# Heads grouped by parity in a memory-attention kernel: scores and the group-0 fold on 64x32 tiles

## The chip, the core and the metric

The kernel runs on one core of a Trainium2 chip. The metric is the device time of one execution, in microseconds (us). TensorE is called PE below (PEld is its weight load), VectorE DVE, ScalarE ACT, GpSimd POOL, and SyncE SP.

## The reference

Attention through 32 memory slots for each of 4 batches and 8 heads, then two dense stages; all of it in float32 (`q`, `k`, `v`: 4 x 8 x 576 x 64, `phi`: 4 x 8 x 576 x 32):

```
a   = softmax(phi, axis=2)                    # over the tokens
k_m = einsum('bhsm,bhsd->bhmd', a, k)         # 32 x 64 for each head
v_m = einsum('bhsm,bhsd->bhmd', a, v)
p   = softmax(q @ k_m^T / 8, axis=-1)         # scores: 576 x 32 for each head
x   = (p @ v_m), heads side by side           # 2304 x 512
x   = ((x @ w_a) * (x @ w_b)) @ w_out         # 512 -> 1536 -> 512
h   = x @ w_in                                # 512 -> 2048
out = (h * sigmoid(1.702 h)) @ w_out2         # 2048 -> 512
```

## The kernel before

The kernel never forms `p @ v_m`. It keeps the attention weights `p` (32 slots x 8 heads = 256 rows for a batch, two halves of 128) and multiplies the values into `w_a` and `w_b`: for each group `g` of 256 columns of F1 (six groups) and each batch, `eff = v_m @ [w_a | w_b]` is made by a fold, and `gated(g, b, u)` multiplies `eff` by `p` (u is a half of the 576 tokens). `proj(g, b, u)` then multiplies by `w_out` and sums over the groups. The second dense stage (L1148, L1349, L1380) follows. The dense matmuls take each float32 operand as a high and a low part in three passes (PASSES).

The heads are cut into NHG = 2 groups of HG = 4. Attention runs over n = 0 to 7, n = 2 b + group. `memory(n)` takes `phi` to the softmax, makes the normalised keys and values of its four heads (L578, `kvn` L592), transposes them (L600) and copies them out of PSUM into two tiles: `bdk` for the keys and `bdv` for the values. Both are written so that a 128-row weight holds one head of 64 rows and 64 rows of zeros; POOL cleared them at the start (L1549). The scores are two groups of matmuls (L622, e = 0 and 1, the two token halves that lie in the upper and lower 64 rows of `qT`), each with four weights of 128 x 32, one for each head, into the four 32-row strips of one PSUM bank. DVE transposes each of the two banks (L628), and `softmax` goes on from there. `queries(n)` loads `q` as one 128-row DMA (L350) and transposes it into `qT`.

The fold of group 0 (`fold0(b)`, L756) has for each half c of the heads four matmuls with weights of 128 x 32 from `bdv`, moving the 512 columns of a decoded weight tile `wab` (the tile of row block r holds heads 2r and 2r + 1). With four heads in order in a half, half c needs the row blocks 2c and 2c + 1. `fold_out` takes the result out: ACT makes the high part (L814), DVE the low part (L816), then the bank is free. The folds of the groups 1 to 5 (`fold(g, pb)`, L800, ten calls of 16 matmuls, two batches each) take a copy of the values (`bdw`, made by `move_memory`) by slices of 64 rows and 32 columns.

PSUM has eight banks in two pools: `bank_m` for the dense work (three banks) and `bank_a` for the attention (five). `warm_up` takes one of `bank_m` at the start and keeps it until the first projections' inputs are there; it fills PE with products of the identity (L1442, the last at L1444). `lend_banks` moves two banks from `bank_a` to `bank_m` when the first half of n = 1 is done, and `close_attention` moves the rest.

The order of all instructions is written by a planner (`Order`): each stream yields the engine, the earliest time and the duration of its next step; the planner takes the step that can start first (in steps of 40 ns, then by priority), on the clocks of its own cost model. `main` has priority 50 and sets the order of the dense work; attention has 10 and up, `warm_up` 99. A step on PE can start 70 ns after its inputs' time (`_plan`), and a step that draws from a pool waits for a bank.

DMAs of `phi`, `kv`, `q` and the packed weights (`raw`) go out on SP in the order FIRST and then by need. A packed weight tile is decoded by ACT (L420) and DVE or POOL (L422 to L435) into `dm` tiles.

Of the kernel before, what the change touches and what calls it, by code (L numbers as in the profile page):

```python
# [176 lines left out]
def tile_mem_attention_moe_moe2(  # L177
# [56 lines left out]
    def slots(pl, n, shape, name, dt=F32):  # L234
# [3 lines left out]
    w2d = dram.tile([F2, DM], F32, name="w2d")  # L238

    banks = [psum.tile([P, 512], F32, name=f"bank{i}") for i in range(8)]  # L240
    bank_m, bank_a = Slots(banks[:3]), Slots(banks[3:])
    raw_s = slots(wp, 2, [P, 512, 2], "raw", U32)
    raw_x = slots(pa, 1, [P, 512, 2], "raw_x", U32)
    raw_p = slots(pa, 1, [P, 512, 2], "raw_p", U32).free[0]
# [14 lines left out]
        g1_m[:, i * G1 * 2 * U:(i + 1) * G1 * 2 * U].rearrange("p (j i t) -> p j i t", j=G1, i=2) for i in range(3)  # L259
    ])  # L260
    p2 = tc.alloc_tile_pool(name="p2", bufs=1)
    bdv_m = p2.tile([P, B * H * M], F32, name="bdv")
    bdv = [
        bdv_m[:, b * H * M:(b + 1) * H * M].rearrange("p (r m) -> p r m", r=H // 2) for b in range(B)
    ]
    gr_s = slots(p2, 3, [P, U], "gr")
    dm_x = slots(p2, 1, [P, 512], "dm_x").free
    dm_s.free += dm_x
    ident = pa.tile([P, P], F32, name="ident")
    zero = pa.tile([P, 1], F32, name="zero")  # L270
    bdk = [pa.tile([P, HG, 2, M], F32, name=f"bdk{i}") for i in range(2)]
    eff_p = pa.tile([P, 2, 2 * CW], F32R, name="eff_p")
    phi_s = slots(pa, 2, [P, HG, C0, M], "phi")
    et_s = slots(pa, 1, [P, C0, SP, 2], "et")
# [40 lines left out]

    def load_heads(dst, src, n, queue=nc.sync):
        b, g = divmod(n, NHG)
        rows_ = src[b, g * HG:(g + 1) * HG].rearrange("h (p c) d -> p h c d", c=SC)
        queue.dma_start(out=dst[0::2], in_=rows_[:, :, :C0, :])
        queue.dma_start(out=dst[1::2, :, :SC - C0, :], in_=rows_[:, :, C0:, :])  # L320

# [3 lines left out]
    def load(x, n):  # L325
        if x == "raw":
            s = yield "slot", raw_of(n)
            if s is raw_p and n >= RX:

                od.mark(s[1], "raw_p")  # L330
                s = yield "slot", raw_of(n)
            srcs, runs = pieces[n][2:]
            m = 512 // len(srcs)
            for i, src in enumerate(srcs):
                dst = s[0][:, i * m:(i + 1) * m, :]
                (nc.scalar if n < 1 else nc.sync).dma_start(
                    out=dst.rearrange("p (n f) w -> p n (f w)", n=runs), in_=src
                )
            size = P * 4096
        else:  # L340
            s = yield "slot", {"phi": phi_s, "kv": kv_s, "q": q_s}[x]
            if x == "kv":
                for i, src in enumerate((k, v)):
                    load_heads(s[0][:, i], src, n)
            elif x == "phi":
                load_heads(s[0], phi, n, nc.scalar if n == 1 else nc.sync)
            else:
                b, g = divmod(n, NHG)
                src = q[b, g * HG:(g + 1) * HG].rearrange("h (p c) d -> (h p) (c d)", c=QC)
                nc.sync.dma_start(out=s[0].rearrange("p c d -> p (c d)"), in_=src)  # L350
            size = HG * S * {"phi": M, "kv": 2 * D, "q": D}[x] * 4
        loaded[x, n] = s
        od.load(s[1], size, x, n)
# [17 lines left out]
        pieces += [(("in", g), i, [rows(w_in, 2 * i, 2, g * G2 * P, G2 * P)], 2) for i in range(2)]  # L371
    pieces += [(("o2", c), 0, [rows(w_o2, c, 1, 0, DM)], 1) for c in range(F2 // P)]
    slots_of = {"o1": whl_s}
    NWB = 10
    decoded = {}

    def decode(first, last, prio):
# [103 lines left out]

    qT_t = {}

    def row(b, h):

        return (h + b % 2) % HG * M

    def queries(n):
        t = yield "mark", "q", n
# [23 lines left out]
    def memory(n):  # L513
# [86 lines left out]
            nc.tensor.transpose(kt[:, i, :], kvn[0][:, i].rearrange("p u d -> p (u d)"), ident)  # L600
        kvn_s.release(kvn, t)
        bk = bdk[n % 2]
        for o in range(2):
            half = slice(o * D, (o + 1) * D)
            t1 = yield from copy(t, bk[half, :, o, :], kt[half, 0, :].rearrange("p (h m) -> p h m", m=M), 128)
        for o in range(2):
            half = slice(o * D, (o + 1) * D)
            t2 = yield from copy(
                t, bdv[b][half, 2 * g:2 * g + 2, o * M:(o + 1) * M],
                kt[half, 1, :].rearrange("p (r o m) -> p r o m", o=2, m=M)[:, :, o, :], 64,  # L610
            )
        bank_a.release(ps, t2)
        od.mark(t2, "bdv", n)

        t = max(t1, (yield "mark", "qT", n))
        qT = qT_t.pop(n)
        sT = yield "slot", sT_s
        ends = []
        for e in range(2):
            t1, ps = yield PE, t, 560, bank_a  # L620
            for h in range(HG):
                nc.tensor.matmul(  # L622
                    ps[0][row(b, h):row(b, h) + M, :U], bk[:, h, e, :], qT[0][:, h, :], start=True, stop=True
                )
            if e == 1:
                qT_s.release(qT, t1)
            t1, _ = yield DVE, max(t1, sT[1]), dve(U)
            nc.vector.transpose(out=sT[0][:, e * U:(e + 1) * U], in_=ps[0][:, :U])  # L628
            bank_a.release(ps, t1)
            ends.append(t1)  # L630
# [56 lines left out]
    def close_attention():  # L687

        for n in range(NU):
            for e in range(2):  # L690
                yield "mark", "attn", n, e
        for c in range(NHG):
            yield "mark", "eff", 0, B - 1, c
        yield "mark", "issued", 0, B - 2, 1
        yield "mark", "raw_p"
        for s in list(bank_a.free):
            bank_m.free.append(s)
        pa.release()
        measured()
        nonlocal py, pz, pv  # L700
        py = tc.alloc_tile_pool(name="py", bufs=1, side="right", reuse_waits="tile")
        pz = tc.alloc_tile_pool(name="pz", bufs=1, side="right", reuse_waits="tile")
        n, nw = 4 * CW, 2 * CW
        big["y0"] = y0 = py.tile([P, 7 * 4 * N2 + 8], F32R, name="y0")
        big["eff_b"] = eff_b = pz.tile([P, NHG * n], F32R, name="eff_b")
        big["whl_b"] = whl_b = pz.tile([P, 4 * G1 * CW], F32R, name="whl_b")
        whl_s.free.append([whl_b, 0.0])
        pv = tc.alloc_tile_pool(name="pw", bufs=1, side="right", reuse_waits="tile")
        plain = pv.tile([P, (NWB * 2 + 4) * CW], F32, name="plain")
        give(wab_s, views(plain, nw, NWB))  # L710

        def effs(*flat):
            return [x.rearrange("p (i f) -> p i f", i=2) for x in flat]

        eff_t.append(effs(*(eff_b[:, c * n:(c + 1) * n] for c in range(NHG))))
        eff_t.append(effs(g1_m[:, :n], g1_m[:, n:2 * n]))
        eff_t.append(effs(g1_m[:, 2 * n:3 * n], y0[:, 2 * G1 * NT:2 * G1 * NT + n]))
        for i in (HI, LO):
            flat = y0[:, i * G1 * NT:(i + 1) * G1 * NT]
            eff_y.append(effs(*(flat[:, c * n:(c + 1) * n] for c in range(NHG))))  # L720
            g1_all.append(flat.rearrange("p (j t) -> p j t", j=G1))
        bdw.extend(x.rearrange("p (r m) -> p r m", r=H // 2) for x in views(plain, H * M, B, NWB * nw))
        od.spawn(8, move_memory())


# [22 lines left out]
    def fold0(b):  # L748
        for c in range(NHG):
            t = yield "mark", "bdv", b * NHG + c  # L750
            for r in range(2):
                t = max(t, (yield "mark", "wab", 0, 2 * c + r, 0))
            t, ps = yield PE, t, 880, bank_m
            for h in range(HG):
                r, k = divmod(h, 2)
                nc.tensor.matmul(  # L756
                    ps[0][row(b, h):row(b, h) + M, :], bdv[b][:, 2 * c + r, k * M:(k + 1) * M],
                    wt["wab", 0, 2 * c + r][0], start=True, stop=True,
                )
            od.spawn(0, fold_out(t, 0, b, c, ps))  # L760

    def move_memory():

        for b in range(B):
            t = 0.0
            for c in range(NHG):
                t = max(t, (yield "mark", "bdv", b * NHG + c))
            t, e = yield {POOL: pool(H * M), ACT: act(H * M)}, t
            dst, src = (x[b].rearrange("p r m -> p (r m)") for x in (bdw, bdv))
            if e == POOL:  # L770
                nc.gpsimd.tensor_copy(dst, src)
            else:
                nc.scalar.activation(out=dst, in_=src, func=AF.Copy)
            od.mark(t, "bdw", b)
        more = [[bdv_m[:, i * 512:(i + 1) * 512], t] for i in range(2)]
        dm_x.extend(more)
        dm_s.free += more

    def fold(g, pb):

# [6 lines left out]
        for i in range(2):  # L787
            for c in range(NHG):
                t, ps[i, c] = yield PE, t - HOP_PE, FOLD if len(ps) == 3 else 0.0, bank_m


        for k in range(NHG):
            for z in (k, 1 - k):
                c, rows_ = k if z == 0 else 1 - k, slice(z * D, (z + 1) * D)
                for h in (z, z + 2):
                    r = 2 * c + h // 2
                    for i in range(2):
                        b = 2 * pb + i
                        o = row(b, h)
                        nc.tensor.matmul(  # L800
                            ps[i, c][0][o:o + M, :], bdw[b][rows_, r, z * M:(z + 1) * M],
                            wt["wab", g, r][0][rows_, :], start=True, stop=True,
                        )
        if pb == B // 2 - 1:
            for r in range(2 * NHG):
                (dm_s if g == 1 else wab_s).release(wt["wab", g, r], t)
# [733 lines left out]
    with tc.manual_schedule():  # L1540
# [4 lines left out]
        for t in [zero, *unused]:  # L1545
            nc.vector.memset(t, 0.0)
        make_identity(nc, ident)
        for t in [*bdk, *bdv]:
            nc.gpsimd.memset(t, 0.0)  # L1549
        n0 = 2 * NHG  # L1550
        od.spawn(0, load_all(FIRST))

# [47 lines left out]
```

## Time and profile before

| what | value |
|---|---|
| median of 3 runs | 774.17 us (773.63 to 2647.37) |
| the profiled execution | 773.3 us |
| its span | 771.5 us |
| PE busy | 760.2 us (99%) |
| PEld busy | 691.2 us (90%) |
| DVE busy | 602.4 us (78%) |
| ACT busy | 382.7 us (50%) |
| POOL busy | 343.2 us (44%) |
| share of PE in the chain that ended last | 93% |

The span is what the trace covers; 1.8 us of the profiled execution lie around it. Busy times are sums over a span of several stages, so the table tells which engine is loaded and not which wait ends last in a stage. A float32 matmul stands in the trace as two MATMUL records, so a group of four matmuls is x8. The end of a matmul is modelled, so the distance from one start to the next is the measure of what a group takes on PE.

### The profile page before, as it was taken

To read this page: it belongs to the slowest core of one execution; us is meant where nothing else is said; L and a number is where in the kernel's file an instruction comes from. 1 tells how busy PE (TensorE), PEld (TensorE's weight loads), DVE (VectorE), ACT (ScalarE), POOL (GpSimd) and SP (SyncE) were. 2 spreads that over 40 slices of the span, in tenths; PEclk is the share of its full clock that TensorE was granted. 3 is DMA by queue.
4 is the path that set the end of the run, shared out by engine and by line. 5 is a ranking of instruction groups with operands and counts; after the bars stand their busy time and mean duration, and the time that the engine had idled before them with its cause. 6 is when DMAs were issued, how large, how long until landed. Compare 5 with 4: busy or idle time off the path is not lost.

```text
span 771.5 us, 14636 instructions
## 1 busy us (share of the span) xinstructions
PE 760.2 (99%) x5448; PEld 691.2 (90%) x5448; DVE 602.4 (78%) x1084; ACT 382.7 (50%) x858; POOL 343.2 (44%) x329
## 2 busy tenths in 40 slices
PE   8999999999999999999999999999999999999997
PEld 7777788999988988989999999999998888889997
DVE  4888989888977897347999878777797887647886
ACT  4567766453434344235565555454554455434442
POOL 1223214444235533226698655433271047654563
PEclk9999999999999999999999999999999999999999
DMA  8956502332221332000012546454679955824421
GB/s 293 329 181 199 162 28 88 106 110 82 83 82 31 107 110 82 1 1 3 1 59 100 184 146 189 157 178 150 219 241 345 294 152 175 265 69 137 137 77 35
DMA packets 70183, 103.97 MB, mean 135 GB/s; under 512 B 5856, under 2 KB 48864, under 8 KB 70112
## 3 DMA queue, kind: packets, MB, share of 16 engines
q1 hardware_dynamic: 64656, 93.64, 38.0%
q10 hardware_dynamic: 5456, 9.41, 3.5%
q8 instruction: 42, 0.69, 0.4%
q14 instruction: 29, 0.24, 0.1%
HBM read 75.24 MB, written 27.79 MB: 134 GB/s over the span
## 4 chain that ended last, share of the span: by engine, by line
PE 93%; DVE 3%; DMA 2%; ACT 1%; issue 1%; SPq 0%; ACTq 0%; DVEq 0%
PE bank L1148 23%; PE bank L840 19%; PE bank L1349 14%; PE bank L1380 10%; PE bank L873 10%; PE bank L896 10%; PE bank L800 2%; DMA phi<-in_phi_dram 1%; PE bank L622 1%; PE bank L578 1%; DMA kv<-in_v_dram 1%; PE bank L497 1%; PE bank L756 1%; ACT et L550 0%; DVE mx L544 0%
## 5 line engine op out<-in xcount | busy, mean ns | idle before, releaser
L304 POOL TENSOR_TENSOR acc<-acc 128x512 f32<-128x512 f32 (+2 forms) x64 | 81.8, 1292 | 81.1 <-ACT y L310 32.3
L304 DVE TENSOR_TENSOR attn<-acc,attn 128x512 fp32r<-128x512 f32 (+2 forms) x93 | 89.4, 981 | 32.1 <-ACT attn L310 32.0
L1190 DVE TENSOR_TENSOR acc<-bank,acc 128x384 f32<-128x384 f32 x168 | 89.4, 552 | 29.8 <-PE bank L1148 19.3
L310 ACT ACTIVATE attn<-acc 128x512 fp32r<-128x512 f32 (+2 forms) x114 | 67.1, 603 | 55.3 <-PE bank L1380 17.9
L853 ACT ACTIVATE gr<-bank 128x288 f32<-128x288 f32 x96 | 38.9, 406 | 76.4 <-PE bank L840 60.4
L1200 ACT ACTIVATE acc<-acc 128x384 f32<-128x384 f32 x96 | 49.0, 522 | 50.8 <-DVE acc L1190 49.8
L304 POOL TENSOR_TENSOR y<-gr,y 128x288 fp32r<-128x288 f32 x44 | 37.5, 855 | 77.6 <-ACT y L310 77.5
L856 DVE TENSOR_TENSOR gr<-bank,gr 128x288 f32<-128x288 f32 x96 | 43.2, 452 | 31.5 <-PE bank L840 26.1
L840 PE MATMUL bank<-attn,eff 128*128 128x288 f32 x384 | 54.6, 297 | 0.0
L840 PEld LDWEIGHTS bank<-attn,eff 128*128 128x128 f32 x384 | 52.0, 188 | 2.9 <-issue 0.9
L873 PEld LDWEIGHTS bank<-g,whl_b 128*128 128x128 f32 x384 | 51.4, 188 | 1.7 <-ACT g L310 1.7
L873 PE MATMUL bank<-g,whl_b 128*128 128x288 f32 x384 | 52.7, 296 | 0.0
L1148 PE MATMUL bank<-attn,y 128*128 128x384 f32 x288 | 52.3, 335 | 0.0
L896 PE MATMUL bank<-y,whl_a 128*128 128x512 f32 (+1 forms) x240 | 51.6, 370 | 0.0
L896 PEld LDWEIGHTS bank<-y,whl_a 128*128 128x128 f32 x240 | 41.4, 188 | 9.8 <-ACT y L310 2.5
L1148 PEld LDWEIGHTS bank<-attn,y 128*128 128x128 f32 x288 | 50.1, 188 | 0.0
L916 DVE TENSOR_TENSOR acc<-bank,acc 128x512 f32<-128x512 f32 (+1 forms) x72 | 38.4, 552 | 13.4 <-PE bank L896 12.8
L304 POOL TENSOR_TENSOR g<-gr,g 128x288 fp32r<-128x288 f32 x28 | 26.3, 941 | 39.2 <-ACT g L310 38.8
L1349 PE MATMUL bank<-wv,attn 128*128 128x512 f32 x180 | 43.2, 394 | 0.0
L1349 PEld LDWEIGHTS bank<-wv,attn 128*128 128x128 f32 x180 | 33.9, 188 | 7.6
L840 PE MATMUL bank<-attn,eff_b 128*128 128x288 f32 x288 | 40.0, 295 | 0.0
L422 POOL TENSOR_SCALAR plain<-plain 128x512 f32<-128x512 f32 x15 | 24.5, 1636 | 34.3 <-ACT plain L420 34.3
(272 smaller groups left out, 1876.4 us busy)
## 6 DMA issues: line engine op xcount, KB each, us to landing
g2d<-acc SPq DMA_DIRECT2D x96, 192.0 KB, 1.9
raw<-in_moe_w_out_dram SPq DMA_DIRECT2D x28, 512.0 KB, 4.3
acc<-g2d SPq DMA_DIRECT2D x10, 1024.0 KB, 5.4
raw<-in_moe_w_in_dram SPq DMA_DIRECT2D x16, 512.0 KB, 3.7
acc<-g2d SPq DMA_DIRECT2D x16, 512.0 KB, 5.4
raw<-in_moe_w_a_dram SPq DMA_DIRECT2D x20, 256.0 KB, 2.8
raw<-in_moe_w_b_dram SPq DMA_DIRECT2D x20, 256.0 KB, 3.1
q<-in_q_dram SPq DMA_DIRECT2D x8, 576.0 KB, 6.4
```

The source lines that it names most:

```text
L304: (nc.gpsimd if e == POOL else nc.vector).tensor_tensor(out=dst, in0=in0, in1=in1, op=op)
L310: nc.scalar.activation(out=hi, in_=src, func=AF.Copy)
L840: nc.tensor.matmul(ps[0][:, :U], e[c][:, sw, i * CW + j * P:i * CW + (j + 1) * P], attn(b, mv, c, u * U, U), start=(n == 0), stop=(n == 3 ...
L853: nc.scalar.activation(out=gr[0], in_=pa_[0][:, :U], func=AF.Copy)
L856: nc.vector.tensor_tensor(out=gr[0], in0=pb[0][:, :U], in1=gr[0], op=ALU.mult)
L873: nc.tensor.matmul(ps[0][:, :U], w[:, sw, j, mb * P:(mb + 1) * P], g1[0][:, j, mv, :], start=(n == 0), stop=(n == 3 * G1 - 1),)
L896: nc.tensor.matmul(ps[0][:, :e - o], w[:, sw, j, mb * P:(mb + 1) * P], g1_all[mv][:, j, o:e], start=(n == 0), stop=(n == 3 * G1 - 1),)
L1148: nc.tensor.matmul(ps[0][:, :N2], w[:, sw, r, :], y[mv][r], start=(n == 0), stop=(n == 5))
L1190: nc.vector.tensor_tensor(out=s[0], in0=ps[0][:, :N2], in1=x[0], op=ALU.add)
L1200: nc.scalar.activation(out=c[0], in_=c[0], func=AF.Gelu_apprx_sigmoid)
L1349: nc.tensor.matmul(ps[i, s][0], b[0][:, sw, c - o, :], wo2[c][:, mv], start=(c == n == 0), stop=(c == 4 * K4 - 1 and n == 2),)
L1380: nc.tensor.matmul(ps[name][0][:, :NB], x[0][:, sw, c, :], moving(b, h // 2 + c, mv), start=(h == c == n == 0), stop=(h > 0 and c == K4 - ...
```

## The change

Head h now belongs to group h mod 2, so group g holds the heads g, g + 2, g + 4, g + 6. A half of the fold's rows then has one head in each row block, always in the same 64 rows. One copy of the keys (`bk`, in both 64-row halves as the transpose leaves it, one copy of 128 x 128) and one of the values (64 x 128 into the half g of `bdv`) replace the two and two copies; the zeros and their clearing go. The scores of both token halves are issued together, eight weights of 64 x 32 into two banks. `fold0` takes for half c the rows 64 c to 64 c + 63 of all four row blocks; the steps of its two halves follow each other, the first with no duration in the planner's model. `fold` of the other groups uses the same helper `fold_head`, so the order of its 16 matmuls differs. The pools are now two and six banks. `q` goes out as four DMAs of 32 rows, since the heads of a group no longer lie side by side. `bdv` is half as wide, which makes room for one more `dm_x` tile from the start (one fewer later) and for an eleventh decoded weight tile (NWB).

```diff
-    bank_m, bank_a = Slots(banks[:3]), Slots(banks[3:])
+    bank_m, bank_a = Slots(banks[:2]), Slots(banks[2:])
...
-    bdv_m = p2.tile([P, B * H * M], F32, name="bdv")
+    bdv_m = p2.tile([P, B * HG * M], F32, name="bdv")
...
-    dm_x = slots(p2, 1, [P, 512], "dm_x").free
+    dm_x = slots(p2, 2, [P, 512], "dm_x").free
...
-    bdk = [pa.tile([P, HG, 2, M], F32, name=f"bdk{i}") for i in range(2)]
+    bdk = [pa.tile([P, HG * M], F32, name=f"bdk{i}") for i in range(2)]
...
-        rows_ = src[b, g * HG:(g + 1) * HG].rearrange("h (p c) d -> p h c d", c=SC)
+        rows_ = src[b].rearrange("(h g) (p c) d -> g p h c d", g=NHG, c=SC)[g]
...
-                src = q[b, g * HG:(g + 1) * HG].rearrange("h (p c) d -> (h p) (c d)", c=QC)
-                nc.sync.dma_start(out=s[0].rearrange("p c d -> p (c d)"), in_=src)
+                src = q[b].rearrange("(h g) (p c) d -> g h p (c d)", g=NHG, c=QC)[g]
+                for h in range(HG):
+                    nc.sync.dma_start(
+                        out=s[0][h * QP:(h + 1) * QP].rearrange("p c d -> p (c d)"), in_=src[h]
+                    )
...
-    NWB = 10
+    NWB = 11
...
-        for o in range(2):
-            half = slice(o * D, (o + 1) * D)
-            t1 = yield from copy(t, bk[half, :, o, :], kt[half, 0, :].rearrange("p (h m) -> p h m", m=M), 128)
-        for o in range(2):
-            half = slice(o * D, (o + 1) * D)
-            t2 = yield from copy(
-                t, bdv[b][half, 2 * g:2 * g + 2, o * M:(o + 1) * M],
-                kt[half, 1, :].rearrange("p (r o m) -> p r o m", o=2, m=M)[:, :, o, :], 64,
-            )
-        bank_a.release(ps, t2)
+        t1 = yield from copy(t, bk, kt[:, 0, :], 128)
+        half = slice(g * D, (g + 1) * D)
+        t2 = yield from copy(t, bdv[b][half].rearrange("p r m -> p (r m)"), kt[half, 1, :], 128)
+        bank_a.release(ps, max(t1, t2))
...
+        t, p0 = yield PE, t, 0.0, bank_a
+        t, p1_ = yield PE, t - HOP_PE, 560, bank_a
+        for h in range(HG):
+            for e, ps in enumerate((p0, p1_)):
+                rows_ = slice(e * D, (e + 1) * D)
+                nc.tensor.matmul(
+                    ps[0][row(h), :U], bk[rows_, h * M:(h + 1) * M], qT[0][rows_, h, :], start=True, stop=True
+                )
+        qT_s.release(qT, t)
         ends = []
-        for e in range(2):
-            t1, ps = yield PE, t, 560, bank_a
-            for h in range(HG):
-                nc.tensor.matmul(
-                    ps[0][row(b, h):row(b, h) + M, :U], bk[:, h, e, :], qT[0][:, h, :], start=True, stop=True
-                )
-            if e == 1:
-                qT_s.release(qT, t1)
-            t1, _ = yield DVE, max(t1, sT[1]), dve(U)
+        for e, ps in enumerate((p0, p1_)):
+            t1, _ = yield DVE, max(t, sT[1]), dve(U)
...
     def fold0(b):
         for c in range(NHG):
             t = yield "mark", "bdv", b * NHG + c
-            for r in range(2):
-                t = max(t, (yield "mark", "wab", 0, 2 * c + r, 0))
-            t, ps = yield PE, t, 880, bank_m
-            for h in range(HG):
-                r, k = divmod(h, 2)
-                nc.tensor.matmul(
-                    ps[0][row(b, h):row(b, h) + M, :], bdv[b][:, 2 * c + r, k * M:(k + 1) * M],
-                    wt["wab", 0, 2 * c + r][0], start=True, stop=True,
-                )
-            od.spawn(0, fold_out(t, 0, b, c, ps))
+            for r in range(2 * NHG):
+                t = max(t, (yield "mark", "wab", 0, r, 0))
+            t, ps = yield PE, t - c * HOP_PE, (0.0, FOLD / 2)[c], bank_m
+            fold_head(c, bdv[b], 0, ps)
+            od.spawn(0, fold_out(t if c else t + FOLD / 2, 0, b, c, ps))
+
+    def fold_head(c, mem, g, ps):
+        half = slice(c * D, (c + 1) * D)
+        for h in range(HG):
+            nc.tensor.matmul(
+                ps[0][row(h), :], mem[half, h, :], wt["wab", g, h][0][half, :], start=True, stop=True
+            )
...
-        more = [[bdv_m[:, i * 512:(i + 1) * 512], t] for i in range(2)]
-        dm_x.extend(more)
-        dm_s.free += more
+        more = [bdv_m, t]
+        dm_x.append(more)
+        dm_s.free.append(more)
...
-        for k in range(NHG):
-            for z in (k, 1 - k):
-                c, rows_ = k if z == 0 else 1 - k, slice(z * D, (z + 1) * D)
-                for h in (z, z + 2):
-                    r = 2 * c + h // 2
-                    for i in range(2):
-                        b = 2 * pb + i
-                        o = row(b, h)
-                        nc.tensor.matmul(
-                            ps[i, c][0][o:o + M, :], bdw[b][rows_, r, z * M:(z + 1) * M],
-                            wt["wab", g, r][0][rows_, :], start=True, stop=True,
-                        )
+        for i in range(2):
+            for c in range(NHG):
+                fold_head(c, bdw[2 * pb + i], g, ps[i, c])
...
-        for t in [*bdk, *bdv]:
-            nc.gpsimd.memset(t, 0.0)
```

## Rows read from the trace of the kernel before

**Rows 1.** Stretches of the span: length, busy time of each engine, clock, DMA share.
```profile
0.00:36.79 36.79, 32.64 (x383) 26.70 (x383) 24.31 (x68) 17.15 (x44) 6.99 (x18) 1.00 0.93 325
36.79:70.39 33.60, 30.54 (x340) 23.57 (x338) 26.73 (x61) 24.05 (x65) 7.93 (x9) 1.00 0.65 199
70.39:108.74 38.35, 38.35 (x406) 30.59 (x402) 35.81 (x79) 26.77 (x76) 11.86 (x9) 1.00 0.37 114
108.74:767.41 658.67, 658.63 (x4332) 610.35 (x4328) 515.17 (x880) 314.70 (x674) 316.44 (x295) 1.00 0.38 122
```

**Rows 2.** PE in order of time: scores, the group-0 fold, and what follows.
```profile
50.43 0.69 PE L622 MATMUL bank<-qT,bdk 128*32 128x288 f32 x8 [0.73 <-ACT bdv L295]
51.06 0.66 PE L558 MATMUL bank<-ident,et 128*128 128x128 f32 x4
...
57.87 0.39 PE L1444 MATMUL bank<-ident 128*128 128x128 f32 x2
...
87.01 1.06 PE L756 MATMUL bank<-wab,bdv 128*32 128x512 f32 x8
87.89 1.28 PE L578 MATMUL bank<-kv,phi 128*32 128x128 f32 x40
...
106.91 1.90 PE L756 MATMUL bank<-wab,bdv 128*32 128x512 f32 x16
108.74 6.65 PE L873 MATMUL bank<-g,whl_a 128*128 128x288 f32 x48
```

**Rows 3.** Lines L622 and L756 from 36.79 us on, and PE's waits there.
```profile
L622 PE MATMUL bank<-qT,bdk x96: 406/406/430, 50.4 to 106.7; 128*32 128x288 f32 x96
...
L756 PE MATMUL bank<-wab,bdv x48: 592/592/617, 56.6 to 108.2; 128*32 128x512 f32 x48
...
PE bank L622 <- ACT bdv L295: 1.3, 2, 0.7
PE bank L622 <- DVE sT L628: 0.7, 1, 0.7
```

**Rows 4.** PE in order of time within one fold of group 1 (L800).
```profile
124.89 0.62 PE L800 MATMUL bank<-dm,plain 64*32 64x512 f32 x2
...
125.35 0.60 PE L800 MATMUL bank<-dm_x,plain 64*32 64x512 f32 x2
...
126.77 0.40 PE L873 MATMUL bank<-g,whl_a 128*128 128x288 f32 x1
```

**Rows 5.** DVE and PE in order of time before the first gated matmul.
```profile
31.16 0.68 DVE L435 SCALAR_TENSOR_TENSOR wab<-raw_x,dm_x 128x512 uint32<-128x512 uint32 x1
...
34.31 0.67 DVE L816 TENSOR_TENSOR eff_p<-bank,eff_p 128x512 fp32r<-128x512 f32 x1
...
35.88 0.46 DVE L304 TENSOR_TENSOR attn<-aT,attn 128x288 fp32r<-128x288 f32 x1
...
36.79 0.64 PE L840 MATMUL bank<-attn,eff_x 128*128 128x288 f32 x3
```

**Rows 6.** DMA issues on SP, a landing time, and ACT's read of that tile.
```profile
L350 SPq DMA_DIRECT2D q<-in_q_dram x8: 334/535/651, 9.2 to 79.4; - x8
...
L1432 SPq DMA_DIRECT2D out_dram<-dm x40: 314/421/1463, 633.0 to 752.1; - x40
...
16.16 0.86 SPq L336 DMA_DIRECT2D raw_x<-in_moe_w_b_dram  x1
...
raw_x<-in_moe_w_b_dram SPq DMA_DIRECT2D x1, 256.0 KB, 6.9
...
25.36 0.67 ACT L420 ACTIVATE dm_x<-raw_x 128x512 f32<-128x512 f32 x1
```

**Rows 7.** One gated bank: filled by PE, emptied by ACT; a later bank's fill.
```profile
42.25 0.56 PE L840 MATMUL bank<-attn,eff_x 128*128 128x288 f32 x3
...
47.87 0.64 PE L840 MATMUL bank<-attn,eff_x 128*128 128x288 f32 x3
...
46.16 0.39 ACT L853 ACTIVATE gr<-bank 128x288 f32<-128x288 f32 x1
```

More of the change, by code (lines that the diff above doesn't have):

```diff
@@ L261, in tile_mem_attention_moe_moe2 @@
     p2 = tc.alloc_tile_pool(name="p2", bufs=1)
-    bdv_m = p2.tile([P, B * H * M], F32, name="bdv")
+    bdv_m = p2.tile([P, B * HG * M], F32, name="bdv")
     bdv = [
-        bdv_m[:, b * H * M:(b + 1) * H * M].rearrange("p (r m) -> p r m", r=H // 2) for b in range(B)
+        bdv_m[:, b * HG * M:(b + 1) * HG * M].rearrange("p (r m) -> p r m", r=HG) for b in range(B)
     ]
     gr_s = slots(p2, 3, [P, U], "gr")
-    dm_x = slots(p2, 1, [P, 512], "dm_x").free
+    dm_x = slots(p2, 2, [P, 512], "dm_x").free
     dm_s.free += dm_x
@@ L482, in tile_mem_attention_moe_moe2, with row @@
     qT_t = {}
-    def row(b, h):
-        return (h + b % 2) % HG * M
+    def row(h):
+        return slice(h * M, (h + 1) * M)
     def queries(n):
@@ L708, in close_attention @@
         pv = tc.alloc_tile_pool(name="pw", bufs=1, side="right", reuse_waits="tile")
-        plain = pv.tile([P, (NWB * 2 + 4) * CW], F32, name="plain")
+        plain = pv.tile([P, (NWB + 1) * 2 * CW], F32, name="plain")
         give(wab_s, views(plain, nw, NWB))
@@ L721, in close_attention @@
             g1_all.append(flat.rearrange("p (j t) -> p j t", j=G1))
-        bdw.extend(x.rearrange("p (r m) -> p r m", r=H // 2) for x in views(plain, H * M, B, NWB * nw))
+        bdw.extend(x.rearrange("p (r m) -> p r m", r=HG) for x in views(plain, HG * M, B, NWB * nw))
         od.spawn(8, move_memory())
@@ L767, in move_memory @@
                 t = max(t, (yield "mark", "bdv", b * NHG + c))
-            t, e = yield {POOL: pool(H * M), ACT: act(H * M)}, t
+            t, e = yield {POOL: pool(HG * M), ACT: act(HG * M)}, t
             dst, src = (x[b].rearrange("p r m -> p (r m)") for x in (bdw, bdv))
```

## Prediction

> **What bounds the kernel now.** I read the stretches first. I cut the span where the PE order shows a change of character: at the first gated matmul (36.79 us), where the gated work of batch 1 begins (70.39), at the last group-0 fold (108.74) and at the last matmul. In the last long stretch PE is busy 658.63 of 658.67 us [rows 1], so nothing but PE sets its length, and whatever reaches 108.74 earlier ends the kernel earlier by the same amount. The third stretch has no PE gap either, but DVE is busy 35.81 of 38.35 us there. The second has 3.06 us without PE work, and in the first DMA is busy 93% of the time [rows 1] while PE mostly multiplies the identity. [...] The change touches work in the first 108.74 us and the inner order of the later folds. So I then read PE in order of time around the scores and the folds, by the distance from one start to the next, and the waits before them.
>
> **The scores.** From 36.79 us on there are 96 records of L622, twelve groups of eight [rows 3], two for each n from 2 to 7. A group takes 0.63 us to the next start [rows 2]; over the twelve the distance lies between 0.48 and 0.69 and sums to some 7.2 us. After the change each n has sixteen records in one go, by eight tiles. Whether the two row halves run beside each other is shown by the later folds, which use just this shape: L800 begins its first records at 124.89 us, the next round at 125.35, and 32 records take 1.88 us to the next line's start [rows 4]. A group of L756 with 512 columns takes 0.88 us and two groups 1.83 [rows 2], so 16 matmuls on 128 x 32 would take some 3.66, and 1.88 is two half-height groups at once. [...] Six times 0.65 is 3.9, so 3.3 us come off PE. If the halves did not overlap, the gain is 0.
>
> **The group-0 fold.** The 48 records of L756 after 36.79 [rows 3] are batches 1 to 3. [...] The six groups stand 0.88 to 1.00 us from the next start where they are alone, and the two of batch 3 take 1.83 together [rows 2]. The batches 2 and 3 (1.87 and 1.83) fall to 1.02 each: 0.85 + 0.81 = 1.7 us. Batch 1 has 1.89 us now, and there I take only 0.2 of the possible 0.87. The planner puts the second half 70 ns after the first, and the warm-up stream, which is ready at any time and in the trace issues its last product (L1444) at 57.87 us, between the two groups of this batch [rows 2], may put its last product between the halves. Bounds: 0 and 0.87. For the same reason another ready stream could split batch 2 or 3 at the cost of one gain; that is in the lower bound. Together PE loses 3.3 + 1.7 + 0.2 = 5.2 us of work before 108.74.
>
> **The copies.** Each n has two copies instead of four. PE waits 1.3 us in two places for the copies of the values (L295) before a score group and 0.7 us for DVE to free a score bank [rows 3]; in the first of these the gap is 0.73 us, right before the score group at 50.43 [rows 2]. With one copy of keys in front of the scores, and six banks for the attention, these 2.0 us may go. They lie in the second stretch, where the chain of n = 2 and 3 decides when gated(0, 1) can start. What is late next is DVE (26.73 of 33.60 us there [rows 1]), so I take half: 1.0 us, bounds 0 and 2.0.
>
> **The start.** Here the change costs. `fold0(0)` can begin only when all four weight tiles are decoded, and `bank_m` has two banks, of which the warm-up holds one. So the first half's result must be taken out before the second half has a bank, and the two are not side by side. The last tile is decoded at 31.84 us (31.16 + 0.68), and DVE ends the result of the half behind it at 34.98 (34.31 + 0.67) [rows 5]: 3.1 us for one half, through PE, ACT and DVE. A second half put behind it is an estimated 2.3 us more (a group of 1.0 and two passes of some 0.65 as DVE's here): 37.3 us. The other input, the first half of n = 1, is ready at 36.34 (35.88 + 0.46), and the first gated matmul stands at 36.79 [rows 5]. So the start moves from 36.8 to some 37.5, a loss of 0.7 us. It could be a gain of 1.0 if the planner orders DVE better (the attention side itself gets shorter by about that, two copies and a score group).
>
> The `q` loads add three issues each on SP. None with 32 rows of 4.6 KB stands in the trace; the nearest rows are the 128-row load of `q` at 0.54 us and the 32-row stores at 0.42 [rows 6]. Two loads of `q` stand ahead of the last weight tiles, so six issues put them (and the keys and values of n = 1 by half of that) back by up to 6 x 0.42 = 2.5 us. The last tile now lands at 23.1 us (16.16 + 6.9) and ACT reads it at 25.36 [rows 6], so 2.3 us of it lie behind other work. I take 0.2 within the 0.7, and 0 to 2.5 as bounds. [...]
>
> **What I cost at nothing.** The clearing by POOL and the smaller `move_memory` copies: POOL is busy 6.99 us of the first 36.79 [rows 1], and nobody waits for the zeros. The eleventh weight tile and the other `dm_x` tile: they let decoding run ahead in a stretch without a PE gap. [...] The fewer banks for `main` are a rival.
>
> **Sum.** 5.2 + 1.0 - 0.7 = 5.5 us. The profiled execution took 773.3 us (1.8 beside its span) and becomes 767.8. The median of the runs shown is 0.9 us above that execution, 774.17, and becomes 768.7; I say 768.6. The case holds between 764.5 (all terms at their good ends) and 771 (split folds, a start later by 1.5, no gain by the copies). This is 0.7%, well under the 2% (15.5 us) that I take as the bound for telling a change from none.
>
> **The rivals.**
>
> DVE takes it back. In the third stretch DVE has only 2.54 us left (38.35 - 35.81 [rows 1]). The two score banks come at once now, and DVE still has to transpose both; where PE is no longer the bound, the attention is late by DVE. Then the gain is at most those 2.5 us, less the 0.7 at the start: 772.4. Against it: the dense work of group 0 that is left at 108.74 needs little of DVE and can be drawn forward, and DVE loses some copies too. [...] Chance 0.12.
>
> The quarters of `q` slow the load. DMA is 93% busy in the first stretch [rows 1]. If each of the first two loads of `q` held the engines for twice as long, 1.8 us more each (590 KB at the 325 GB/s of the stretch [rows 1]), and the slack were used by the planner elsewhere, the start loses 3.6 instead of 0.7 us: 771.6. Chance 0.07. [...]
>
> It doesn't do what it says: other steps of the planner come between the halves of every fold, and the row halves of the scores don't overlap, since their matmuls alternate between the halves where L800's came in fours. Then only the copies are gained and the start is lost: 774. Chance 0.06.
>
> Slower than before, by the banks of the dense work. `main` has three banks instead of four until the warm-up ends and four instead of five until the attention is closed. A gated bank that begins to fill at 42.25 us is emptied by 46.55 (46.16 + 0.39) [rows 7], 4.3 us later. A group of six matmuls fills a bank in 0.8 us, so with four banks a holding time over 3.2 us makes PE wait. If all of the some 38 dense groups from 70.39 to the close of the attention held a bank for 4.3 us, each would take 4.3 / 4 = 1.08 instead of 0.8: 38 x 0.28 = 10.6 us, so 773.3 + 10.6 - 5.5 = 778.4, about 779 on the median's scale. It decides from a mean holding time of 3.2 us on. Against it: with attention work between, the third bank after the one above is asked for only at 47.87 us [rows 7], when it is long free, and I found no place in the trace where four banks would have been too few. Chance 0.08.
>
> It goes better: the chain of n = 2 and 3 is shorter by two waits and a score group, and the start comes earlier too. Then 762.5 to 764. Chance 0.07.
>
> **How the numbers follow.** The forecast has 0.60, the five others 0.12, 0.07, 0.06, 0.08 and 0.07. The range from 764.0 to 774.5 holds the forecast, the DVE case, the quarters and half of the case without effect, about 0.82. All cases but the ends of the last two lie within 2% of 774.17 (758.7 to 789.7): faster 0.02, same 0.96, slower 0.02.
>
> **What the profile after would show.** Right: L622's successor with x16 (n each) and some 0.65 us to the next start; the fold of batches 2 and 3 as x16 with about 1.0; ten L800 folds still at 1.9; the first gated matmul at 37 to 38 us; the last long stretch without a PE gap and with its length unchanged within 1 us. Wrong: score groups of 1.2 us, fold halves apart by another line, PE gaps with gated or projection matmuls waiting for ACT or DVE (banks) or for attention rows (DVE), a first gated matmul after 39 us. The planner orders everything anew, and a different order of DVE work before 70 us is what could most easily move the time by a few us either way.

## The result: slower, and the profile after

The changed kernel takes 778.9 us (median of 20 runs, 773.76 to 782.53), the kernel before 773.75 in the same series: ratio 1.0062, 95% interval 1.0049 to 1.0076. That is 0.6% slower, inside the 2% in which I put 0.96. It is outside the forecast range of 764.0 to 774.5, and the time moved up where it was forecast to move down. The profiled execution of the changed kernel took 781.35 us, with a span of 779.5 and a mean granted clock of 0.992.

The stretches of the changed kernel, cut at its first gated matmul, where the gated work of batch 1 begins, at the end of its last group-0 fold and at the last matmul (columns as in [rows 1]):

```profile
0.00:42.76 42.76, 34.95 (x401) 29.09 (x401) 25.56 (x72) 17.85 (x43) 5.73 (x11) 1.00 0.95 266
42.76:82.69 39.93, 33.05 (x402) 28.08 (x401) 30.35 (x65) 25.84 (x68) 12.41 (x11) 0.94 0.78 214
82.69:116.49 33.80, 33.36 (x342) 28.40 (x340) 28.18 (x60) 23.23 (x63) 13.20 (x10) 0.92 0.31 92
116.49:775.44 658.95, 658.87 (x4336) 610.35 (x4328) 512.95 (x878) 315.27 (x677) 312.09 (x295) 1.00 0.38 122
```

The last long stretch is 658.95 us against 658.67 [rows 1], again without a PE gap. It starts 7.75 us later (116.49 against 108.74), and the span is 8.0 us longer, so the whole loss lies before it. The first gated matmul is at 42.76 instead of 36.79: 6.0 us, and past the 39 us that the prediction gave as a sign of being wrong. The other 1.8 us arise between there and the end of the last fold: PE has 7.3 us without work (6.88 in the second stretch, 0.44 in the third) against 3.06 before [rows 1], and is busy 2.5 us less (66.4 against 68.9).

PE in order of time, the lines that answer to [rows 2] and [rows 5]:

```profile
38.67 0.63 PE L500 MATMUL bank<-ident,q 128*128 128x128 f32 x4 [1.59 <-DMA q<-in_q_dram]
...
42.76 0.65 PE L830 MATMUL bank<-attn,eff_x 128*128 128x288 f32 x3
...
60.15 0.63 PE L500 MATMUL bank<-ident,q 128*128 128x128 f32 x4 [2.78 <-DMA q<-in_q_dram]
...
61.48 1.79 PE L863 MATMUL bank<-g,whl_a 128*128 128x288 f32 x6
...
69.74 1.04 PE L863 MATMUL bank<-g,whl_a 128*128 128x288 f32 x6
...
72.97 1.84 PE L863 MATMUL bank<-g,whl_a 128*128 128x288 f32 x12
74.74 0.72 PE L620 MATMUL bank<-qT,bdk 64*32 64x288 f32 x16
75.39 0.66 PE L561 MATMUL bank<-ident,et 128*128 128x128 f32 x4
...
81.95 1.09 PE L500 MATMUL bank<-ident,q 128*128 128x128 f32 x4 [2.96 <-DMA q<-in_q_dram]
82.69 3.23 PE L830 MATMUL bank<-attn,eff 128*128 128x288 f32 x12
...
115.47 1.09 PE L759 MATMUL bank<-wab,bdv 64*32 64x512 f32 x16
116.49 6.94 PE L863 MATMUL bank<-g,whl_a 128*128 128x288 f32 x48
```

What the change was made of works: the scores of one n take 0.65 us to the next start (75.39 - 74.74) and the fold of a batch 1.02 (116.49 - 115.47), both to the hundredth what the prediction had. But PE now waits for `q`. The two largest waits of PE in the whole attention, each with total, number and longest:

```profile
PE bank L500 <- DMA q<-in_q_dram: 9.1, 6, 3.0
PE bank L581 <- DVE sm L646: 1.9, 1, 1.9
```

Before, no wait of PE for `q` was in the list. A wait of nearly 3 us also costs afterwards: after 60.15 six records of L863 take 1.79 us where six take 1.04 at 69.74, and after 81.95 twelve of L830, of the same shape, take 3.23 where twelve of L863 take 1.84 at 72.97. Stretches of 2 us around these two waits (columns as in [rows 1], the clock third from the right) show it:

```profile
58.00:60.00 2.00, 0.00 (x0) 0.00 (x0) 0.00 (x0) 0.69 (x2) 0.00 (x0) 1.00 0.96 231
60.00:62.00 2.00, 1.85 (x11) 1.89 (x12) 0.35 (x1) 0.60 (x1) 0.00 (x0) 0.67 0.98 269
62.00:64.00 2.00, 2.00 (x11) 1.98 (x10) 1.97 (x7) 0.68 (x2) 0.00 (x0) 0.50 0.95 271
64.00:66.00 2.00, 2.00 (x27) 1.49 (x26) 1.12 (x2) 1.95 (x9) 0.00 (x0) 0.98 1.04 314
...
82.00:84.00 2.00, 2.00 (x9) 2.00 (x10) 0.00 (x0) 0.60 (x1) 0.00 (x0) 0.50 1.02 314
84.00:86.00 2.00, 2.00 (x11) 1.98 (x10) 0.00 (x0) 0.77 (x2) 0.00 (x0) 0.50 0.98 303
86.00:88.00 2.00, 2.00 (x11) 2.00 (x10) 1.53 (x6) 1.10 (x3) 0.11 (x1) 0.51 0.92 220
```

PE does nothing from 58 to 60 us, and the granted clock is at 0.50 of full speed in the 2 us from 62 on; after the wait before 81.95 it is at 0.50 and 0.51 for 6 us.

DMA moves less at full load. From 8 to 36 us, the kernel before and then the changed one (the last three columns are clock, DMA share and GB/s):

```profile
8.00:36.00 28.00, 25.19 (x305) 19.55 (x302) 21.87 (x57) 15.17 (x41) 4.60 (x5) 1.00 1.03 369
```

```profile
8.00:36.00 28.00, 23.12 (x315) 18.55 (x308) 19.22 (x50) 12.02 (x32) 4.65 (x5) 1.00 1.04 288
```

The engines are as busy (1.04 and 1.03) and carry 288 GB/s instead of 369. The issues on SP, those of `q` and the last half of the last weight tile (answer to [rows 6]):

```profile
9.16 1.83 SPq L351 DMA_DIRECT2D q<-in_q_dram  x4
...
14.79 2.91 SPq L351 DMA_DIRECT2D q<-in_q_dram  x4
...
21.92 0.33 SPq L336 DMA_DIRECT2D raw_x<-in_moe_w_b_dram  x1
```

That last issue was at 16.16 us [rows 6] and is 5.8 us later.

### The profile page after: what moved, and what is told of

Read it like the earlier page. It is cut to its first block, busy times and chain, and to the rows that moved or that the text cites. A ratio compares the mean times of both kernels' runs of the same rounds, so it can differ in the third digit from the quotient of the medians.

```text
span 779.5 us, 14681 instructions
## 1 busy us (share of the span) xinstructions
PE 760.2 (98%) x5466; PEld 695.9 (89%) x5466; DVE 597.5 (77%) x1073; ACT 382.2 (49%) x849; POOL 343.4 (44%) x327
## 4 chain that ended last, share of the span: by engine, by line
PE 91%; DMA 6%; SPq 2%; DVE 1%; issue 0%; ACT 0%; DVEq 0%
PE bank L1138 22%; PE bank L830 19%; PE bank L1339 14%; PE bank L1370 10%; PE bank L863 10%; PE bank L886 10%; DMA q<-in_q_dram 5%; PE bank L759 3%; SPq L351 1%; PE bank L500 1%; DMA kv<-in_k_dram 1%; PE bank L581 1%; SPq L320 0%; PE bank L620 0%; SPq L319 0%
## 5 line engine op out<-in xcount | busy, mean ns | idle before, releaser
L830 PE MATMUL bank<-attn,eff 128*128 128x288 f32 x384 | 56.0, 303 | 0.0
L830 PEld LDWEIGHTS bank<-attn,eff 128*128 128x128 f32 x384 | 53.7, 194 | 1.9 <-ACT plain L423 0.8
L863 PEld LDWEIGHTS bank<-g,whl_b 128*128 128x128 f32 x384 | 51.4, 188 | 1.7 <-ACT g L310 1.7
L863 PE MATMUL bank<-g,whl_b 128*128 128x288 f32 x384 | 52.7, 296 | 0.0
L830 PE MATMUL bank<-attn,eff_b 128*128 128x288 f32 x288 | 40.0, 295 | 0.0
L830 PEld LDWEIGHTS bank<-attn,eff_b 128*128 128x128 f32 x288 | 38.9, 188 | 0.2
```

The source lines that it names most:

```text
L830: nc.tensor.matmul(ps[0][:, :U], e[c][:, sw, i * CW + j * P:i * CW + (j + 1) * P], attn(b, mv, c, u * U, U), start=(n == 0), stop=(n == 3 ...
L863: nc.tensor.matmul(ps[0][:, :U], w[:, sw, j, mb * P:(mb + 1) * P], g1[0][:, j, mv, :], start=(n == 0), stop=(n == 3 * G1 - 1),)
```

## The experiments

Theory 1 after the result: the loss is the load of `q` in four DMAs of 32 rows. Rival 2: the fewer banks for the dense work, or the new order. Within theory 1 three causes were open: the number of issues on SP, the few rows of a transfer, or where these rows lie. The medians are beside runs of the kernel before on the same chip (773.6 to 773.8).

**e1: q in one DMA, everything else as changed.**

```diff
-                src = q[b].rearrange("(h g) (p c) d -> g h p (c d)", g=NHG, c=QC)[g]
-                for h in range(HG):
-                    nc.sync.dma_start(
-                        out=s[0][h * QP:(h + 1) * QP].rearrange("p c d -> p (c d)"), in_=src[h]
-                    )
+                src = q[b, g * HG:(g + 1) * HG].rearrange("h (p c) d -> (h p) (c d)", c=QC)
+                nc.sync.dma_start(out=s[0].rearrange("p c d -> p (c d)"), in_=src)
```

> The changed kernel with q loaded in one 128-row DMA as before (of four neighbouring heads, so the wrong queries meet the keys; the work on the engines is the same). Theory 1 (the four loads of 32 rows make q late: PE waits 9.1 us for q in six places, and the clock falls after the long waits): no PE wait for q over 0.3 us, first gated matmul by 38.5 us instead of 42.8, no stretch at the half clock, and the prediction's sum comes out: 767 to 769.5. Rival 2 (banks, or the new order of DVE and PE work, is what costs): 774 or more, first gated matmul after 40 us.

769.73 us, ratio 0.9953 (0.9939 to 0.9967). The profiled run has a clock of 1.0 and its DMA moves 374 GB/s from 8 to 36 us. So the rest of the change gains 4.0 us and the loads cost 9.2. The time is 0.2 above the expected range, the first gated matmul is at 37.83 us as expected, and the expected "no wait over 0.3" was missed: two waits for `q` remain, 1.8 us in all. I take it that the rest of the attention is earlier now and meets them.

**e2: the kernel before with q in four DMAs of 32 neighbouring rows.**

```diff
-                src = q[b, g * HG:(g + 1) * HG].rearrange("h (p c) d -> (h p) (c d)", c=QC)
-                nc.sync.dma_start(out=s[0].rearrange("p c d -> p (c d)"), in_=src)
+                src = q[b, g * HG:(g + 1) * HG].rearrange("h (p c) d -> h p (c d)", c=QC)
+                for h in range(HG):
+                    nc.sync.dma_start(
+                        out=s[0][h * QP:(h + 1) * QP].rearrange("p c d -> p (c d)"), in_=src[h]
+                    )
```

> The kernel before with nothing but q loaded as four DMAs of 32 rows each. Theory 1: the whole loss is here, so it costs some 10 us: 780 to 787, with PE waits for q of 6 us or more. Rival 2: the loads hide as they did, 774 to 776.

778.56 us, ratio 1.0068 (1.0053 to 1.0083). The split alone makes the old kernel 4.8 us slower, less than the 10 expected, and the waits for `q` are 4.6 us in three places instead of 9.1 in six. I take it that it meets a longer attention there; no run shows that by itself. The DMA engines are as full as in the changed kernel and again move less than 369 GB/s:

```profile
8.00:36.00 28.00, 24.12 (x319) 17.97 (x308) 20.40 (x52) 14.17 (x38) 4.60 (x5) 1.00 1.02 296
```

**e3: the kernel before with q in four DMAs of 128 rows and a quarter of the columns.**

```diff
-                nc.sync.dma_start(out=s[0].rearrange("p c d -> p (c d)"), in_=src)
+                for o, e in ((0, 5), (5, 10), (10, 14), (14, 18)):
+                    nc.sync.dma_start(out=s[0][:, o:e, :], in_=src[:, o:e, :])
```

> The kernel before with q loaded as four DMAs of 128 rows, each a quarter of the columns: the same number of issues, but all rows. If the number of issues on SP is what delays (about 0.4 us each, 1.2 to 2 us a load), it is within 2 us of the run with 32 rows each. If the 32 rows of a transfer are what is slow, it stays at 774 to 776 and only the run with 32 rows is slower.

774.02 us, ratio 1.0004 (0.9996 to 1.0013): no difference. The trace of this run on SP:

```profile
9.16 1.85 SPq L351 DMA_DIRECT2D q<-in_q_dram  x4
...
14.18 2.85 SPq L351 DMA_DIRECT2D q<-in_q_dram  x4
...
18.80 0.33 SPq L336 DMA_DIRECT2D raw_x<-in_moe_w_b_dram  x1
```

The issues take SP just as long as in the changed kernel (1.83 and 2.91), and it costs nothing, although the last half of the last weight tile is issued 2.6 us later than before (16.16 [rows 6]). So 2.6 of the 5.8 us by which that issue is late in the changed kernel are harmless here. The number of issues is not the cause.

**e4: the changed kernel with three and five banks.**

```diff
-    bank_m, bank_a = Slots(banks[:2]), Slots(banks[2:])
+    bank_m, bank_a = Slots(banks[:3]), Slots(banks[3:])
```

> The changed kernel with three and five banks as before. Theory 1: still 777 to 781, PE still waits 7 us or more for q. Rival 2 in the form of the banks: 774 or less, and the first gated matmul 2 us or more earlier.

784.7 us, ratio 1.0145 (1.0131 to 1.0158): slower by another 5.8 us, and outside what both theories expected. PE's wait for `q` shrinks to 0.7 us, against what theory 1 expected, while PE waits for other things (ACT's `et` 5.2 us in four places). The first gated matmul is at 44.53 us, later and not earlier. The bank theory as I had it, too few for the dense work, is contradicted: giving that work one more bank, taken from the attention, makes it worse.

**e5: the changed kernel, the four loads of 32 rows each going to every fourth row.**

```diff
-                        out=s[0][h * QP:(h + 1) * QP].rearrange("p c d -> p (c d)"), in_=src[h]
+                        out=s[0][h::HG].rearrange("p c d -> p (c d)"), in_=src[h]
...
-                ps[0][:, :k * P].rearrange("p (c h s) -> p c h s", h=HG, s=QP), k * P,
+                ps[0][:, :k * P].rearrange("p (c s h) -> p c h s", h=HG, s=QP), k * P,
```

> The changed kernel with its four DMAs of 32 rows, but each to every fourth of the 128 rows instead of to 32 neighbouring ones (the copy of q out of PSUM then reads the heads at a step of four; the result is the same). Issues on SP and bytes are those of the change. If what is slow is a transfer into 32 neighbouring rows (the DMA engines are busy 1.04 of the time from 8 to 36 us and move 288 GB/s instead of 369), this takes the loss away: 768.5 to 771, 340 GB/s or more there, PE waits for q of 2.5 us or less. Rival (few rows in a transfer, wherever they lie): 776 to 780 and below 300 GB/s.

769.52 us, ratio 0.9947 (0.9935 to 0.996). Same issues, same bytes, same number of rows; only the place of the rows differs (and with it the step at which the copy out of PSUM reads), and 9.4 us come back. It is as fast as e1 with its single DMA (769.73), so in the changed kernel too the issues cost nothing. From 8 to 36 us it moves less than the 340 GB/s expected, but its engines have room:

```profile
8.00:36.00 28.00, 25.07 (x336) 20.61 (x327) 21.92 (x59) 14.08 (x36) 4.95 (x5) 1.00 0.97 328
```

**e6: the kernel before with the same spread loads** (the two lines of e5 on top of e2).

> The kernel before with q in four DMAs of 32 rows, each to every fourth row. If the place of the rows decides: 773.5 to 775, as with 128 rows each. If the number of rows decides: 777 to 780, as with 32 neighbouring rows.

774.5 us, ratio 1.0011 (1.0002 to 1.002). The split that costs 4.8 us with neighbouring rows costs 0.9 when the rows are spread.

**e7: q in one DMA (as e1) and three and five banks (as e4).**

> The changed kernel with q in one DMA (of neighbouring heads, so the wrong queries) and three and five banks. With the slow loads the three and five banks cost 6 us more than two and six. If that was the attention waiting for a pair of score banks out of the three that are left to it, it is there without the slow loads too: 774 to 778. If it came only together with late loads: 768 to 771.

778.41 us, ratio 1.0058 (1.0046 to 1.0071): 8.7 us slower than e1, 0.4 above the expected range. The bank split matters without the slow loads too. `lend_banks` takes two of the five, so the attention has three. In the trace PE waits for ACT's `et` in four places, 6.2 us in all:

```profile
PE bank L558 <- ACT et L550: 6.2, 4, 2.2
PE bank L600 <- ACT kvn L592: 1.3, 1, 1.3
```

In e1 this `et` wait is not in the list from the first fold on. That the pair of score banks, taken together out of three, is what makes the planner order it so was not shown by itself.

**e8: e5 with q loaded ahead of phi and kv from n = 2 on.**

```diff
-        od.spawn(2, load_all([(x, n) for n in range(2, NU) for x in ("phi", "kv", "q")]))
+        od.spawn(2, load_all([(x, n) for n in range(2, NU) for x in ("q", "phi", "kv")]))
```

> The changed kernel with q to every fourth row and, from n = 2 on, q loaded ahead of phi and kv instead of behind them. With one DMA for q PE still waited 1.8 us in two places for q. If these waits lie on the path, this gains up to 1.5 us over the same kernel without the new order: 767.5 to 769. If the transposes of q only stand in PE's order where phi would be waited for next, it gains nothing or loses 1 us.

767.51 us, ratio 0.9921 (0.9909 to 0.9934): 6.1 us faster than the kernel before, the best of all. It is not by shorter waits for `q` (2.3 us in two places, 2.0 in e5): between its first gated matmul and its last fold it takes 61.84 us where e5 takes 66.05, with 1.43 instead of 3.43 us without PE work.

```profile
39.62:101.46 61.84, 60.41 (x732) 51.45 (x731) 56.58 (x128) 45.26 (x124) 19.49 (x17) 1.00 0.60 188
```

**e9: e5 with three and five banks and one bank lent.**

```diff
-    bank_m, bank_a = Slots(banks[:2]), Slots(banks[2:])
+    bank_m, bank_a = Slots(banks[:3]), Slots(banks[3:])
...
         yield "mark", "attn", 1, 0
-        for _ in range(2):
+        for _ in range(1):
```

> The changed kernel with q to every fourth row, three and five banks, and one bank lent instead of two, so that both pools have four after the loan as in the change, while the dense work has two free banks before it instead of one. If the start is lost because the second half of the first fold waits for the first half's bank (second group at 35.54 us, first gated matmul at 38.18), the two groups stand together by 32.5 us, the first gated matmul comes by 37, and the time falls by about 1: 768 to 769. If three and five banks cost because the attention is left with three after the loan, nothing of the 9 us of that run comes back here. Rival (the five banks at the start are what costs): 772 or more.

772.74 us, ratio 0.9982 (0.9973 to 0.9991). The start does what was expected: both halves of the first fold are one group and the first gated matmul is at 36.39 us instead of 38.18.

```profile
31.11 1.64 PE L759 MATMUL bank<-wab,bdv 64*32 64x512 f32 x16
...
36.39 0.64 PE L830 MATMUL bank<-attn,eff_x 128*128 128x288 f32 x3
```

But the time is 3.2 us longer than e5's, where the rival had put it (772 or more): five banks at the start, or the order of work that comes with them, cost more than the earlier start brings. Beside e7 (the same five banks, two lent) 5.7 of the 8.7 us are back, which fits the attention's need of a fourth bank after the loan. The trace shows part of the 3.2: between its first gated matmul and the end of its last fold PE has 4.64 us without work, against 3.43 in e5, and the clock falls here too, after waits of only 1.56 and 0.44 us. The forty records of L581 at 72.00 us take 2.29 us to the next start, those at 64.68 took 1.23:

```profile
72.00:74.00 2.00, 2.00 (x40) 1.77 (x40) 2.00 (x5) 1.84 (x4) 0.65 (x1) 0.50 1.05 353
```

**e10: e9 with the load order of e8.**

> The same with q loaded ahead of phi and kv from n = 2 on. If both gains add up: 766 to 767.2, below the 767.5 of the new load order alone. If the start is not on the path once q comes first: 767.5.

773.71 us, ratio 0.9996 (0.9987 to 1.0005). Missed by 6: the gains don't add up, and why this order of work is 6 us worse than e8 is open. In the trace PE waits 2.1 us for `q` before 29.85 us, and the mean clock of the first 38 us is 0.96 (1.00 from 38 to 104 us); that alone is not 6 us.

**e11: e5 with the scores as two steps of the planner again.**

```diff
-        t, p0 = yield PE, t, 0.0, bank_a
-        t, p1_ = yield PE, t - HOP_PE, 560, bank_a
-        for h in range(HG):
-            for e, ps in enumerate((p0, p1_)):
-                rows_ = slice(e * D, (e + 1) * D)
...
+        for e in range(2):
+            t1, ps = yield PE, t, 560, bank_a
+            rows_ = slice(e * D, (e + 1) * D)
+            for h in range(HG):
```

> The changed kernel with q to every fourth row and the scores of the two token halves as two steps of the planner again (weights of 64 x 32 as in the change, everything else as in the change). By the prediction's term of 3.3 us for the scores: 771.5 to 773.5. If two score groups cost little because PE is filled with other work or DVE is what the chain waits for: 769 to 770.5.

772.6 us, ratio 0.9984 (0.9975 to 0.9992): 3.1 us slower than e5. The term for the scores was 3.3. One group alone still takes some 0.62 us to the next start, with half the rows of before (102.58 to 103.20), so it is the issue of both halves together that gains.

**e12: the kernel before with q in two DMAs of 64 neighbouring rows.**

```diff
-                nc.sync.dma_start(out=s[0].rearrange("p c d -> p (c d)"), in_=src)
+                for o in (0, P // 2):
+                    half = slice(o, o + P // 2)
+                    nc.sync.dma_start(out=s[0][half].rearrange("p c d -> p (c d)"), in_=src[half])
```

> The kernel before with q in two DMAs of 64 neighbouring rows. [...] If the rate only grows with the number of rows in a transfer, it lies in the middle or below: 774 to 776 and 320 GB/s or more.

778.83 us, ratio 1.0063 (1.005 to 1.0077), as slow as four DMAs of 32 (778.56), and above the 774 to 776 of a rate that grows with the number of rows. Again the engines are full and move less, 302 GB/s against the 320 or more of that case:

```profile
8.00:36.00 28.00, 23.35 (x283) 17.44 (x279) 19.97 (x51) 14.04 (x38) 4.59 (x5) 1.00 1.05 302
```

## Why the prediction was wrong, point by point

**The bound.** Right: the last stretch follows PE alone, and all that was won or lost before it went into the time one to one (7.75 us at its start, 8.0 in the span).

**The scores and the fold.** Right in mechanism, and near in size. No run of the kernel before shows the 0.65 us of the scores of one n or the 1.02 of a fold, from which the terms 3.3 and 1.7 come: they were my estimate. The changed kernel shows 0.65 and 1.02 us in their place, and e11 3.1 us for the scores against 3.3. In e5, from the first gated matmul to the end of the last fold:

```profile
38.18:104.23 66.05, 62.62 (x741) 52.07 (x739) 58.25 (x125) 48.65 (x131) 25.43 (x21) 1.00 0.57 176
```

PE is busy 62.62 us there, against 68.89 (30.54 + 38.35 [rows 1]): 6.3 us less where I had 5.2. Batch 1 gained too (one group of x16 at 58.67 us in e5), which I had taken at 0.2 of 0.87. The order of L800 costs nothing to speak of: the last long stretch of the changed kernel is 0.3 us longer.

**The copies.** Wrong in the net: of the 1.0 us of waits that were to go, nothing remains as a gain. In e5 the time without PE work there is 3.43 us, against 3.06 [rows 1]; the old waits are gone and others (`q`, `phi`, `et`) stand in their place.

**The start, and the step that failed.** The step that failed is the term for the loads of `q`. I costed the four loads as issues on SP, "up to 6 x 0.42 = 2.5 us", and took 0.2. In its place the runs show 9.2 us (the change against e1) to 9.4 us (against e5), and not by the issues: e3 and e5 show that these cost nothing; e2, e12, e5 and e6 show that the loads into neighbouring rows hold the DMA engines longer. From 8 to 36 us these are busy 1.02 and 1.05 of the time for 296 and 302 GB/s with neighbouring rows (e2, e12), and 0.97 for 328 and 325 with spread ones (e5, e6). In the same window the changed kernel, busy 1.04 of the time, moves 81 GB/s less over 28 us, 2.3 MB, or 6.1 us of work at 369 GB/s; about three loads of `q` fall in it, so a load holds the engines an estimated 2 us longer.

I had this as the rival of the quarters, with 1.8 us a load and a chance of 0.07. The size for a load was about right, but the price of the rival, 771.6, was too small, for two reasons. It counted only the two loads ahead of the first gated matmul, while PE waits for `q` in six places, the last before 81.95 us. And it left out what happens on PE: the planner has put the transposes of `q` at fixed places in PE's order, PE stands before them (9.1 us), and the clock falls to 0.50 after the two gaps of nearly 3 us (2.78 and 2.96). The forecast has no term for the clock. In the kernel before it is 1.00 in all four stretches [rows 1]; in the changed one it is 0.94 in the second and 0.92 in the third.

How much of the loss is the clock? In the profiled execution PE works for some 9.4 us at a clock of about 0.50 (from 60.7 to 64 and from 82 to 88). At 1.00 the same work takes half of that at the least, so the clock costs it at most an estimated 4.7 us of the 11.8 between 781.35 and the median of e5. The 20 executions of the changed kernel point the same way: the three with a mean clock of 1.000 took 773.76 to 774.81 us, the others, at 0.989 to 0.998, 776.45 to 782.53. So about half of the 9.4 us between the median and e5 (4.7, the median less 774.2) goes with the lower clock. But an execution with a lower clock may also have had longer waits, so this half is no price of the clock alone; no kernel was made to tell the two apart.

What decided is the place of the rows of a transfer, and the times agree on it in three points: 64 neighbouring rows are as slow as 32 (778.83 and 778.56), 32 rows at every fourth are not (774.5), and e5 takes the loss away (769.52 against 778.9). Why neighbouring rows are slower is not shown by any row of a trace. The nearest rows that I went by were of stores and of 128 rows. And I overlooked nearer ones: the kernel before loads `phi`, keys and values in pairs of transfers to every second row (L319 and L320), 64 rows each, within the stretch that moves 369 GB/s.

**The first fold behind one bank.** It happens as told (second group at 35.54 us in e5, first gated matmul at 38.18, 1.4 us later where I had 0.7). But it does not decide the time as I took it to: e9 puts the first gated matmul at 36.39 and is slower, e8 has it at 39.62 and is faster. Both change something else too, so the 1.4 us is not priced by itself. The order of the three goes with PE's time without work from there to the last fold: 1.43 us in e8, 3.43 in e5, 4.64 in e9.

**The rivals.** DVE did not take the gain back: in e5 the way from the first gated matmul to the last fold is 5.9 us shorter, with 6.3 us less PE work. More banks for the dense work did not help: taken from the attention, they cost 5.8 us (e4) and 8.7 (e7), and 3.2 with one bank lent (e9). What the dense work would do with more banks at no cost to the attention was not tried. That this rival stood at about 779 and the change at 778.9 is chance: with q in one DMA and the banks of the change e1 takes 769.73. That the change doesn't do what it says is refuted by the rows (0.65 and 1.02 us).

The sum, with the slow loads undone: 6.3 us less PE work, 0.4 more without work and 1.4 at the start make 4.5 us; the median of e5 is 4.1 below that of the kernel before. The forecast of 5.5 was 1.4 us too high for that part.

## What to carry to other kernels

When a change splits or moves a DMA, ask first which rows of the SBUF each transfer touches: with `q` loaded into 32 or 64 neighbouring rows at a time the DMA engines moved 296 and 302 GB/s here where the kernel before moved 369, and a step in the partition index (every fourth row) cost 0.9 us where neighbouring rows cost 4.8. Look at GB/s beside the busy share of the DMA engines: here an equal share (1.04 and 1.03) with fewer GB/s (288 and 369) was a slower kind of transfer, not less work. And look at the clock after a wait of PE: after its gaps of 2.78 and 2.96 us the changed kernel ran PE at a clock of about 0.50 for some 3 and 6 us, so these waits were paid twice.

## What I had not expected of the hardware

The four issues of a load of `q` took SP 1.83 to 2.91 us where the one of the kernel before took 0.33 to 0.65, and in e3 (1.85 and 2.85 us for the first two loads) that was without any effect on the time (ratio 1.0004). The same kernel spread from 773.76 to 782.53 us over 20 executions, where the kernel before mostly stays within 1.6 us. Its three fastest executions are those with a mean clock of 1.000. Why the clock falls in some executions and not in others is open. Long waits for `q` are not needed for a spread: the longest in e1 is 1.0 us, and its six runs lie 4.0 us apart (768.6 to 772.57), while the five runs of e5 lie within 0.6 us.
